# Two MLP layers after a retention layer: the split of the weights' sums put one slot behind the sums, and parts of two x sums put two slots later

## The chip, the cores and the metric

The kernel runs on one core of a Trainium2 chip. The metric is the device time of that core in microseconds (us); smaller is better.

## The reference, cut to what matters

```python
x = retention(q, k, v)                    # 1536 tokens x 512, state over time, 8 heads
h = x @ w_in;   x = softplus(h) @ w_out   # first MLP, d_ff 2048
h = x @ w_in2;  g = s * relu(h)**2 + b
out = g @ w_out2                          # second MLP
```

All data are float32 for the caller. The kernel keeps float32 accuracy on TensorE by splitting each operand into a high part and a low part (hi + lo) and adding three products: hi x hi, hi x lo, lo x hi.

## The kernel before

The kernel has a retention stage, a first MLP layer whose early steps run between the retention's steps, and a second MLP layer. The change concerns the second layer and the passage into it. The tokens are three tiles j = 0, 1, 2 of 512; d_ff is 16 blocks of 128, taken as 8 pairs p. The order of the instructions on every engine is the order in which the program issues them, and an engine takes its instructions strictly in that order.

**Weights.** A weight block arrives packed; `split_w` unpacks one half of it (index 0: w_in, 1: w_out) in steps. DVE runs L286, L290, L295 and L301; ACT runs Square (L293, output `wm`) ahead of L301; then `split` (L109) makes the parts: ACT copies `wh` (L111) and POOL subtracts `wl` (L114). The generator stops between steps, and `go(work, n)` runs n further ones.

**Sums of weights.** For the pairs 1 to 7 the layer's first product over tiles 0 and 1 is made in Strassen's way with seven half-sized products. It needs four sums of the weights (`sums_w`: four POOL instructions on tile `ws`, L320), split into `sh` (ACT, L111) and `sl` (POOL, L114), and sums of x (`sum_x`, DVE, L431 and L435, in place in `xa`), split by `parts_x` (ACT copy at L442 or L445, POOL subtraction at L448).

**Slots.** `halves` lists the pieces in the order in which they are taken: for each pair two w_in halves, the sums, and two w_out halves, five pieces. Each call of `part(p)` takes the next one. Pair 0 is `plain(0)`, six slots, one for each tile and block; this document names them (0,0), (0,1), (1,0), (1,1), (2,0), (2,1). A slot issues the 12 matmuls of the first product (`all_of`), then `flat` and `bend` (ACT: Relu, Square at L491, L492, copy `gh` at L111; POOL: `gl` at L114), then two steps of the piece, then the matmuls and additions given to it (`accs`), then `sum_x` and `parts_x`, then the rest of the piece. In (1,0) `accs` is `end`: the first layer's last accumulation and `take_last`, in which DVE adds (L416), ACT copies (L418) and DVE subtracts (L420). After that the accumulator banks are free, and (1,1) issues the second layer's first accumulation (`acc_2`, L510).

The pairs 1 to 7 are `second(p)`, in six groups of matmuls; the first five had a piece each. This document calls them s1 to s6. In s1 `kept` copies a PSUM bank to tile `p1` on ACT (L468), and `joined` adds on DVE (L479) and applies Relu on ACT (L480). In s2 `kept` fills `p5` and `u2`. `six` issues six matmuls of a half-sized product. There are three banks for these results, `h`, `y` and `third`, and a new product waits for the copy or addition that empties its bank.

Of the kernel before, what the change touches and what calls it, by code (L numbers as in the profile page):

```python
# [47 lines left out]
def tile_retention_mlps(ctx: ExitStack, tc: tile.TileContext, qk, kv, w1, w2, sb, consts, out):  # L48
# [19 lines left out]
    def bank(pool, tag):  # L68
        return pool.tile([P, 512], F32, tag=tag, name=tag)
# [39 lines left out]
    def split(hi, lo, src, hi_eng, lo_eng):  # L109
        if hi_eng is nc.scalar:  # L110
            nc.scalar.activation(hi, src, AF.Copy)  # L111
        else:
            hi_eng.tensor_copy(hi, src)
        lo_eng.tensor_tensor(out=lo, in0=src, in1=hi.bitcast(F32), op=ALU.subtract)  # L114
# [158 lines left out]
    def split_w(w, i, pause):  # L273

        wh = wp.tile([P, DM], F32R, tag=f"wh{i}", name=f"wh{i}")
        wl = wp.tile([P, DM], F32R, tag=f"wl{i}", name=f"wl{i}")
        t = raw_t.pop((w, i))
        lw, hw = t[:, :, 0], t[:, :, 1]

        if bank_2:  # L280
            x = bank_2[w < NF and 1 - i].bitcast(U32)
        else:
            x = (un[:, i] if spare() else word()).bitcast(U32)
        m = dp.tile([P, DM], F32, tag="wm", name="wm")

        nc.vector.tensor_scalar(  # L286
            out=x, in0=hw, scalar1=3, scalar2=0x3FFFFFF8, op0=ALU.logical_shift_left, op1=ALU.bitwise_and
        )
        yield
        nc.vector.scalar_tensor_tensor(  # L290
            out=x, in0=hw, scalar=cu[:, 0:1], in1=x, op0=ALU.bitwise_and, op1=ALU.bitwise_or
        )
        nc.scalar.activation(m, hw.bitcast(F32), AF.Square)  # L293
        yield
        nc.vector.scalar_tensor_tensor(  # L295
            out=x, in0=lw, scalar=cu[:, 1:2], in1=x, op0=ALU.logical_shift_right, op1=ALU.bitwise_or
        )
        load_next()
        yield

        nc.vector.scalar_tensor_tensor(  # L301
            out=m, in0=m, scalar=TINY_SQ, in1=x.bitcast(F32), op0=ALU.is_ge, op1=ALU.mult
        )
        m_t[w, i] = m
        if pause:
            yield
        split(wh, wl, m, nc.scalar, nc.gpsimd)
        w_t[w, i] = (wh, wl)

    def sums_w(w):  # L310

        a, b = m_t[w, 0], m_t[w + 1, 0]
        t = late.tile([P, 4, KH], F32, tag="ws", name="ws")
        for o, x, y, op in (
            (0, b[:, :KH], b[:, KH:], ALU.add),
            (1, t[:, 0], a[:, :KH], ALU.subtract),
            (2, a[:, :KH], b[:, :KH], ALU.subtract),
            (3, a[:, KH:], t[:, 1], ALU.subtract),
        ):
            nc.gpsimd.tensor_tensor(out=t[:, o], in0=x, in1=y, op=op)  # L320
            if o == 1:
                yield
        hi = late.tile([P, 4, KH], F32R, tag="sh", name="sh", bufs=2)
        lo = late.tile([P, 4, KH], F32R, tag="sl", name="sl", bufs=2)
        yield
        split(hi, lo, t, nc.scalar, nc.gpsimd)
        s_t[w] = (hi, lo)


    steps = [(0, g, j, f4) for g in range(NG) for j in range(NTILE) for f4 in range(FG)]  # L330
# [94 lines left out]
    def sum_x(k):  # L425

        (b11, b21), (b12, b22) = ((xa[j][:, 0:2], xa[j][:, 2:4]) for j in (0, 1))
        if k == 3:
            for c, tag in enumerate(("p1", "p5")):
                t = late.tile([P, TT], F32, tag=tag, name=tag)  # L430
                nc.vector.tensor_tensor(out=t, in0=b22[:, c], in1=b12[:, c], op=ALU.subtract)  # L431
                x3.append(t)
            return
        to, x, y = {1: (b11, b12, b11), 2: (b22, b22, b11), 4: (b12, b21, b22)}[k]
        nc.vector.tensor_tensor(out=to, in0=x, in1=y, op=ALU.subtract)  # L435
        x_t[k] = to
# [46 lines left out]
    def flat(ps):  # L483
        c = next_t()
        nc.scalar.activation(c, ps, AF.Relu)
        return c
# [55 lines left out]
        ),  # L542
    )
    for w in range(NF, 2 * NF, 2):
        halves += [(w, 0), (w + 1, 0)] + [(w, 2)] * (w > NF) + [(w, 1), (w + 1, 1)]
    RAWS = 4
    loads, splits = iter([x for x in halves if x[1] < 2]), iter(halves)
    nxt = [next(splits)]
# [6 lines left out]
    def split_next(s):  # L555
        x = nxt[0]
        if x is None or (x[0] < NF + 2 and x[1] < 2 and s < slot_free(*x)) or (NF + 2 <= x[0] and s < NS):
            return iter(())
        assert x[0] >= NF or s + 1 <= first_use(*x) or s <= min(SB, first_use(*x)), (s, x)
        nxt[0] = next(splits, None)  # L560
        if x[1] == 2:
            return sums_w(x[0])
        return split_w(*x, pause=True)

    def go(work, n):
        for _ in range(n):
            next(work, None)
# [57 lines left out]
    with tc.manual_schedule():  # L625
# [119 lines left out]
        def part(p):  # L745
            return split_next(NS + p) if p < PAIRS - 1 else iter(())
# [5 lines left out]
        def plain(p):  # L752

            w = NF + 2 * p

            def slot(j, half, to, accs, sums=(), parts=()):
                work = part(p)
                all_of(to, w_t[w + half, 0], j)
                c = flat(to)
                bend(c, p, half, j)  # L760
                go(work, 2)
                accs()
                for k in sums:
                    sum_x(k)
                for k in parts:
                    parts_x(k)
                go(work, 3)

            def end():
                for banks in (FIRST, SECOND):  # L770
                    acc_mm(NS - 1, banks)
                    take_last(banks)

            def sums_0():
                acc_2(p, 0, 1)
                take(p, 0)

            slot(0, 0, bank(ps_h, "h"), lambda: acc_mm(NS - 3, FIRST + SECOND), sums=(2,), parts=(1,))
            slot(0, 1, bank(ps_y, "y"), lambda: acc_mm(NS - 2, FIRST + SECOND), sums=(4,), parts=(2,))
            slot(1, 0, bank_2[1], end)  # L780
            slot(1, 1, bank(ps_h, "h"), lambda: acc_2(p, 0, 0), parts=(4,))
            slot(2, 0, bank_2[1], sums_0)
            slot(2, 1, bank(ps_y, "y"), lambda: None, parts=(3,))

        def second(p):

            w = NF + 2 * p
            (ah, al), (bh, bl), (sh, sl) = w_t[w, 0], w_t[w + 1, 0], s_t[w]
            a11, a12 = (ah[:, :KH], al[:, :KH]), (ah[:, KH:], al[:, KH:])
            a22 = bh[:, KH:], bl[:, KH:]  # L790
            s1, s2, s3, s4 = ((sh[:, k], sl[:, k]) for k in range(4))
            b11, b21 = ((xh[0][:, k : k + 2], xl[0][:, k : k + 2]) for k in (0, 2))
            b22 = xh[1][:, 2:4], xl[1][:, 2:4]
            t1, t2, t3, n4 = (x_t[k] for k in (1, 2, 3, 4))

            one, other, third = bank(ps_h, "h"), bank(ps_y, "y"), bank_2[1]

            work = part(p)
            six(one, a11, b11, True)
            p1 = kept(one, "p1")  # L800
            six(third, a12, b21, True)
            c11 = joined(third, p1)
            go(work, 2)
            acc_2(p - 1, 1, 0)
            bend(c11, p, 0, 0)
            go(work, 3)

            work = part(p)
            six(other, s1, t1, True)
            p5 = kept(other, "p5")  # L810
            six(one, s2, t2, False)
            u2 = kept(one, "u2")
            go(work, 2)
            acc_2(p - 1, 1, 1)
            take(p - 1, 1)
            go(work, 3)

            work = part(p)
            six(other, s4, b22, False)
            c12 = joined(other, u2)  # L820
            six(one, s3, t3, False)
            c22 = joined(one, p5)
            go(work, 2)
            acc_2(p - 1, 2, 0)
            bend(c12, p, 0, 1)
            bend(c22, p, 1, 1)
            go(work, 3)

            work = part(p)
            six(one, a22, n4, False)  # L830
            c21 = flat(one)
            go(work, 2)
            acc_2(p - 1, 2, 1)
            take(p - 1, 2)
            bend(c21, p, 1, 0)
            go(work, 3)

            work = part(p)
            all_of(third, (ah, al), 2)
            ha = flat(third)  # L840
            go(work, 2)
            acc_2(p, 0, 0)
            bend(ha, p, 0, 2)
            go(work, 3)

            other = bank(ps_y, "y")
            all_of(other, (bh, bl), 2)
            hb = flat(other)
            for banks in (FIRST, SECOND) if p == PAIRS - 1 else (FIRST + SECOND,):
                acc_2(p, 0, 1, banks)  # L850
                take(p, 0, banks)
            bend(hb, p, 1, 2)

        go(work, 4)
        act_3(NS - 1)
# [82 lines left out]
```

## Time and profile before

| | |
|---|---|
| median of 3 runs | 591.48 us (591.41 to 592.08) |
| profiled execution, time | 591.23 us |
| its span, first to last instruction | 589.2 us |
| mean granted TensorE clock | 0.988 |
| PE busy | 569.9 us, 97% of the span |
| DVE, ACT, POOL busy | 419.4, 316.6, 237.6 us |

The granted clock is a share of TensorE's full 2.4 GHz; 0.5 is 1.2 GHz. PE is TensorE's matmuls, PEld its weight loads, DVE VectorE, ACT ScalarE, POOL GpSimd. Times in the views count from the span's start; L111 is line 111 of the kernel. A row of a timeline gives start, duration, engine, line, operation, output and inputs, count, and in brackets the idle time ahead of it and what ended that.

### The profile page before, as it was taken

Reading aid. Unit: us, or ns where it says so; the run is one execution under the profiler, and the core shown is the slowest. Engines: PE = TensorE matmul, PEld = TensorE weight load, DVE = VectorE, ACT = ScalarE, POOL = GpSimd, SP = SyncE. Lnnn points to the kernel's source line nnn. Section 1 sums busy time; section 2 is a strip of 40 time slices with the busy share of each in tenths; the row PEclk is TensorE's granted clock in tenths of the full one; section 3 lists DMA queues with packets and bytes.
Section 4 is the critical chain, followed back from the end, with each engine's and each line's share of the span. In section 5 each row is a group of like instructions: output and inputs, shape, how many; then the busy total and the mean of one; then the engine's idle time right before and its main releaser. Section 6 shows DMA issues by size and latency. Waiting matters only on the chain.

```text
span 589.2 us, 7951 instructions
## 1 busy us (share of the span) xinstructions
PE 569.9 (97%) x2986; PEld 467.4 (79%) x2986; DVE 419.4 (71%) x626; ACT 316.6 (54%) x570; POOL 237.6 (40%) x197
## 2 busy tenths in 40 slices
PE   8999999999999999999999498999999999999997
PEld 7777778888888888888888376888888888888885
DVE  4898767779799997999868385739485766653324
ACT  3655564443323323333535577867767676767460
POOL 3547632121111120111535868474746474735030
PEclk9999999999999999999999798999999999999999
DMA  8985122222122221222212032213122221000005
GB/s 329 416 310 202 52 71 73 72 73 73 36 72 71 72 72 37 71 72 71 73 36 65 7 106 71 78 32 98 48 71 72 71 72 60 14 1 0 1 0 214
DMA packets 14869, 50.57 MB, mean 86 GB/s; under 512 B 1776, under 2 KB 1776, under 8 KB 14832
## 3 DMA queue, kind: packets, MB, share of 16 engines
q1 hardware_dynamic: 14832, 50.08, 24.8%
q8 instruction: 23, 0.38, 0.3%
q14 instruction: 14, 0.11, 0.1%
HBM read 46.93 MB, written 3.15 MB: 85 GB/s over the span
## 4 chain that ended last, share of the span: by engine, by line
PE 82%; DMA 5%; DVE 4%; POOL 3%; ACT 3%; issue 2%; SPq 0%; DVEq 0%; POOLq 0%
PE acc L510 21%; PE acc L396 20%; PE h L349 12%; PE y L349 9%; PE h L454 6%; PE y L462 3%; PE third L462 3%; PE y L454 3%; DMA qk<-qk 3%; PE y L189 2%; DMA raw<-w 2%; PE third L454 1%; PE s L173 1%; POOL gl L114 1%; POOL wl L114 1%
## 5 line engine op out<-in xcount | busy, mean ns | idle before, releaser
L114 POOL TENSOR_TENSOR wl<-wm,wh 128x512 fp32r<-128x512 f32 x64 | 83.3, 1302 | 230.9 <-ACT wh L111 230.8
L519 DVE TENSOR_TENSOR xa<-acc,xa 128x512 f32<-128x512 f32 x84 | 52.4, 683 | 81.6 <-PE acc L510 81.5
L114 POOL TENSOR_TENSOR gl<-c,gh 128x512 fp32r<-128x512 f32 x48 | 63.2, 1316 | 80.8 <-ACT gh L111 67.2
L362 ACT ACTIVATE t<-t 128x512 f32<-128x512 f32 x48 | 30.2, 630 | 102.9 <-DVE t L356 102.8
L510 PE MATMUL acc<-wh,gh 128*128 128x512 f32 x192 | 76.1, 396 | 8.6 <-DVE xl L420 8.6
L510 PE MATMUL acc<-wh,gl 128*128 128x512 f32 x192 | 75.6, 394 | 0.0
L396 PE MATMUL acc<-gh,wh 128*128 128x512 f32 x192 | 75.6, 394 | 0.0
L396 PE MATMUL acc<-gl,wh 128*128 128x512 f32 x192 | 74.8, 390 | 0.0
L111 ACT ACTIVATE wh<-wm 128x512 fp32r<-128x512 f32 x64 | 39.8, 622 | 52.2 <-DVE wm L301 52.2
L396 PE MATMUL acc<-gh,wl 128*128 128x512 f32 x192 | 58.1, 389 | 0.0
L382 DVE TENSOR_TENSOR gl<-t,gh 128x512 fp32r<-128x512 f32 x40 | 51.7, 1293 | 1.2 <-ACT gh L378 1.2
L510 PE MATMUL acc<-wl,gh 128*128 128x512 f32 x192 | 52.5, 389 | 0.0
L510 PEld LDWEIGHTS acc<-wh,gh 128*128 128x128 f32 x192 | 36.5, 190 | 17.5 <-issue 9.0
L293 ACT ACTIVATE wm<-raw 128x512 f32<-128x512 f32 x64 | 42.2, 660 | 8.5 <-POOL wl L114 8.4
L349 PE MATMUL h<-xh,wh 128*128 128x512 f32 x112 | 44.7, 399 | 2.2 <-DVE t L366 1.7
L349 PE MATMUL h<-xl,wh 128*128 128x512 f32 x112 | 43.7, 390 | 0.0
L396 PEld LDWEIGHTS acc<-gh,wh 128*128 128x128 f32 x192 | 36.0, 188 | 8.8 <-DVE xa L406 1.0
L510 PEld LDWEIGHTS acc<-wh,gl 128*128 128x128 f32 x192 | 36.6, 191 | 7.5
L510 PEld LDWEIGHTS acc<-wl,gh 128*128 128x128 f32 x192 | 36.2, 188 | 7.6
L396 PEld LDWEIGHTS acc<-gh,wl 128*128 128x128 f32 x192 | 36.0, 188 | 7.6
L396 PEld LDWEIGHTS acc<-gl,wh 128*128 128x128 f32 x192 | 36.1, 188 | 7.2
L492 ACT ACTIVATE c<-c,sbt 128x512 f32<-128x512 f32 x48 | 39.2, 816 | 1.6
(178 smaller groups left out, 1239.1 us busy)
## 6 DMA issues: line engine op xcount, KB each, us to landing
raw<-w SPq DMA_DIRECT2D x64, 512.0 KB, 3.7
qk<-qk SPq DMA_DIRECT2D x12, 512.0 KB, 8.1
kv<-kv SPq DMA_DIRECT2D x12, 512.0 KB, 8.0
out<-xa SPq DMA_DIRECT2D x12, 256.0 KB, 2.1
cst<-consts SPq DMA_DIRECT2D x1, 518.0 KB, 4.1
cst<-consts SPq DMA_DIRECT2D x1, 256.0 KB, 5.9
sbt<-sb SPq DMA_DIRECT2D x1, 1.0 KB, 9.8
```

What stands on the lines that cost most here:

```text
L111: nc.scalar.activation(hi, src, AF.Copy)
L114: lo_eng.tensor_tensor(out=lo, in0=src, in1=hi.bitcast(F32), op=ALU.subtract)
L293: nc.scalar.activation(m, hw.bitcast(F32), AF.Square)
L349: nc.tensor.matmul(ps, w[:, cc * P : (cc + 1) * P], r[j][:, cc, :], start=i == 0, stop=i == len(ops) - 1)
L362: nc.scalar.activation(l_t[s], l_t[s], AF.Softplus)
L382: (eng or nc.vector).tensor_tensor(out=gl, in0=l_t.pop(s), in1=gh.bitcast(F32), op=ALU.subtract)
L396: nc.tensor.matmul(acc_t[la, g, j][cc], *ops[i], start=f4 == 0 and i == 0, stop=ends(s) and i == 2)
L454: nc.tensor.matmul(ps, w[a][:, k * P : (k + 1) * P], x[b][:, k], start=start and i == 0, stop=i == len(ops) - 1, skip_group_check=True,)
L462: nc.tensor.matmul(ps, w[a][:, k * P : (k + 1) * P], (xh, xl)[b][j][:, k], start=i == 0, stop=i == len(ops) - 1)
L492: nc.scalar.activation(c, c, AF.Identity, scale=sbt[:, 0:1], bias=sbt[:, 1:2])
L510: nc.tensor.matmul(acc_t[1, p, j][cc], *ops[i], start=half == 0 and i == 0, stop=half == 1 and i == 2)
L519: nc.vector.tensor_tensor(out=dst, in0=ps, in1=dst, op=ALU.add)
```

## The change

The split of the sums becomes a piece of its own, so a pair has six pieces, and s6 of `second(p)` gets a piece as well. `sum_x(4)` moves from (0,1) to (0,0), behind `sum_x(2)`. `parts_x(2)` moves from (0,1) to (1,1), and `parts_x(4)` from (1,1) to (2,0). The two halves of the third x sum are kept in the tiles `p5` and `u2` instead of `p1` and `p5`.

```diff
 def sums_w(w):
             nc.gpsimd.tensor_tensor(out=t[:, o], in0=x, in1=y, op=op)
             if o == 1:
                 yield
+        s_t[w] = t
+
+    def split_sums(w):
         hi = late.tile([P, 4, KH], F32R, tag="sh", name="sh", bufs=2)
         lo = late.tile([P, 4, KH], F32R, tag="sl", name="sl", bufs=2)
+        split(hi, lo, s_t[w], nc.scalar, nc.gpsimd)
+        s_t[w] = (hi, lo)
         yield
-        split(hi, lo, t, nc.scalar, nc.gpsimd)
-        s_t[w] = (hi, lo)
...
-            for c, tag in enumerate(("p1", "p5")):
+            for c, tag in enumerate(("p5", "u2")):
...
-        halves += [(w, 0), (w + 1, 0)] + [(w, 2)] * (w > NF) + [(w, 1), (w + 1, 1)]
+        halves += [(w, 0), (w + 1, 0)] + [(w, 2), (w, 3)] * (w > NF) + [(w, 1), (w + 1, 1)]
...
         if x[1] == 2:
             return sums_w(x[0])
+        if x[1] == 3:
+            return split_sums(x[0])
...
-            slot(0, 0, bank(ps_h, "h"), lambda: acc_mm(NS - 3, FIRST + SECOND), sums=(2,), parts=(1,))
-            slot(0, 1, bank(ps_y, "y"), lambda: acc_mm(NS - 2, FIRST + SECOND), sums=(4,), parts=(2,))
+            slot(0, 0, bank(ps_h, "h"), lambda: acc_mm(NS - 3, FIRST + SECOND), sums=(2, 4), parts=(1,))
+            slot(0, 1, bank(ps_y, "y"), lambda: acc_mm(NS - 2, FIRST + SECOND))
             slot(1, 0, bank_2[1], end)
-            slot(1, 1, bank(ps_h, "h"), lambda: acc_2(p, 0, 0), parts=(4,))
-            slot(2, 0, bank_2[1], sums_0)
+            slot(1, 1, bank(ps_h, "h"), lambda: acc_2(p, 0, 0), parts=(2,))
+            slot(2, 0, bank_2[1], sums_0, parts=(4,))
             slot(2, 1, bank(ps_y, "y"), lambda: None, parts=(3,))
...
+            work = part(p)
             other = bank(ps_y, "y")
             all_of(other, (bh, bl), 2)
             hb = flat(other)
+            go(work, 2)
             for banks in (FIRST, SECOND) if p == PAIRS - 1 else (FIRST + SECOND,):
                 acc_2(p, 0, 1, banks)
                 take(p, 0, banks)
             bend(hb, p, 1, 2)
+            go(work, 3)
```

## Rows read from the trace of the kernel before

**Rows 1.** Stretches: us; busy PE, PEld, DVE, ACT, POOL; clock; DMA share; GB/s.

```profile
44.00:48.00 4.00, 3.41 (x20) 2.62 (x22) 3.83 (x8) 2.43 (x7) 3.24 (x3) 1.00 0.71 281
...
365.10:368.70 3.60, 3.60 (x10) 2.80 (x9) 1.39 (x3) 1.49 (x3) 2.46 (x2) 0.53 0.46 146
372.00:556.00 184.00, 184.00 (x813) 152.38 (x812) 111.14 (x170) 128.09 (x205) 99.22 (x82) 1.00 0.15 49
```

**Rows 2.** Timeline of PE, 336 to 372 us.

```profile
337.47 0.77 PE L510 MATMUL acc<-wh,gh 128*128 128x512 f32 x1 [8.58 <-DVE xl L420]
...
342.16 0.39 PE L462 MATMUL third<-xh,wh 128*128 128x512 f32 x1
...
358.00 0.50 PE L454 MATMUL h<-x2h,sh 128*128 128x512 f32 x1 [0.72 <-ACT p L468]
...
364.33 0.50 PE L454 MATMUL y<-xh,sh 128*128 128x512 f32 x1 [1.95 <-ACT p L468]
...
368.77 0.39 PE L510 MATMUL acc<-wh,gh 128*128 128x512 f32 x1
```

**Rows 3.** Timeline of ACT, 320 to 336 us.

```profile
322.23 0.63 ACT L111 ACTIVATE wh<-wm 128x512 fp32r<-128x512 f32 x1 [1.22 <-DVE wm L301]
...
324.89 0.63 ACT L111 ACTIVATE gh<-c 128x512 fp32r<-128x512 f32 x1
...
330.76 1.06 ACT L111 ACTIVATE sh<-ws 128x1024 fp32r<-128x1024 f32 x1 [4.29 <-POOL ws L320]
331.73 0.58 ACT L485 ACTIVATE c<-third 128x512 f32<-128x512 f32 x1
...
334.94 1.07 ACT L418 ACTIVATE xh<-acc 128x512 fp32r<-128x512 f32 x2
```

**Rows 4.** Timeline of DVE, 319 to 326 us.

```profile
319.52 1.22 DVE L435 TENSOR_TENSOR xa<-xa,xa 128x1024 f32<-128x1024 f32 x1
...
322.11 2.11 DVE L435 TENSOR_TENSOR xa<-xa,xa 128x1024 f32<-128x1024 f32 x1
```

**Rows 5.** Timeline of POOL, 319 to 331 us.

```profile
319.56 2.32 POOL L114 TENSOR_TENSOR gl<-c,gh 128x512 fp32r<-128x512 f32 x1 [1.90 <-ACT gh L111]
...
326.59 1.29 POOL L114 TENSOR_TENSOR gl<-c,gh 128x512 fp32r<-128x512 f32 x1
327.83 0.73 POOL L320 TENSOR_TENSOR ws<-wm 128x256 f32<-128x256 f32 x1
```

**Rows 6.** Tile x1l: ns min/median/max of one, first and last start.

```profile
L448 POOL TENSOR_TENSOR x1l<-xa,x1h x2: 1288/1780/2273, 321.9 to 323.1; 128x512 fp32r<-128x512 f32 x2
```

**Rows 7.** Timeline of ACT, 356 to 366 us (s1 and s2 of pair 1).

```profile
357.36 0.60 ACT L468 ACTIVATE p<-h 128x512 f32<-128x512 f32 x1 [0.54 <-POOL xl L448]
358.71 0.63 ACT L480 ACTIVATE c<-c 128x512 f32<-128x512 f32 x1 [0.76 <-DVE c L479]
...
363.70 0.58 ACT L468 ACTIVATE p<-y 128x512 f32<-128x512 f32 x1
```

**Rows 8.** Timeline of ACT, 434 to 470 us (a later pair).

```profile
433.59 0.63 ACT L480 ACTIVATE c<-c 128x512 f32<-128x512 f32 x1
...
436.71 0.62 ACT L491 ACTIVATE c<-c 128x512 f32<-128x512 f32 x1
```

**Rows 9.** Timeline of DVE, 448 to 468 us.

```profile
448.78 2.48 DVE L519 TENSOR_TENSOR xa<-acc,xa 128x512 f32<-128x512 f32 x4 [3.76 <-PE acc L510]
...
464.15 0.68 DVE L479 TENSOR_TENSOR c<-h,p 128x512 f32<-128x512 f32 x1
...
466.25 0.76 DVE L295 SCALAR_TENSOR_TENSOR word<-raw,cu,word 128x512 uint32<-128x512 uint32 x1
467.14 0.69 DVE L301 SCALAR_TENSOR_TENSOR wm<-wm,word 128x512 f32<-128x512 f32 x1
```

**Rows 10.** Chain that ended last, 448 to 462 us: start, us, what.

```profile
460.08 1.36 PE y L454 x6
```

## The prediction

> **What bounds the kernel now.** I read the page's engine totals first, then PE's waits, then the granted clock by stretches, and then each engine's timeline where PE waits. PE is the bound: from 372 to 556 us it is busy all the time at full clock [rows 1], and nothing that shortens another engine there can pay. What is left lies in the passage into the second layer, where PE waits three times [rows 2]: 8.58 us ahead of 337.47, 0.72 ahead of 358.00 and 1.95 ahead of 364.33. After the first and the third wait it runs for a while at half clock. A sequence of 12 matmuls takes 2 x 1.36 = 2.72 us at full clock [rows 10]; from 337.47 to 342.16 it took 4.69, and from 364.33 to 368.77 it took 4.44 [rows 2], with a granted clock of 0.53 in the second stretch [rows 1]. So 1.97 and 1.72 us more. Those five items, 14.9 us, are all that this change can win; the time to lose is in the pairs, where nothing is idle now.
>
> Why PE waits: the first time it wants an accumulator bank that `take_last` empties. Its ACT copy (334.94) stands behind the four instructions of the third slot's bend and a Square, and these stand behind `sh`, which had kept ACT idle for 4.29 us, waiting for `ws` on POOL [rows 3]. The second time `p1` is not written yet, since POOL still reads the third x sum in that same tile: 0.54 us of ACT's idle time [rows 7]. The third time ACT writes `p5` only at 363.70 [rows 7], since its queue has the `sh` of the next pair ahead of it, with its wait for `ws`.
>
> **The change, part by part.**
>
> *First wait.* `sh` is now issued behind the third slot's bend, so these instructions run while ACT would wait for `ws`. From 331.73 to 334.94, 3.21 us, leaves the path behind `sh` [rows 3]; the Square goes with it, because the w_out half is taken a slot later. Against this stands how late `ws` and so `sh` become. `sum_x(4)` now stands ahead of L295 and L301 of the piece in (0,0). Its price: 1.22 or 2.11 us [rows 4]. The traces tell why two sizes: the first sum began 0.04 us before POOL's `gl`, kept its 1.22, and `gl` took 2.32 instead of 1.29; the other began 0.2 us after the first `x1l`, was held back until that ended (1.29), and then the second `x1l`, next on POOL, was held to 2.27 [rows 4 to 6]. So the one that began first runs on, and at its end the waiting one goes before its neighbour's next. `gl` waits when `sum_x(4)` comes, so it should go first, to 319.56 + 2.32 = 321.88, and `sum_x(4)` should end at 321.88 + 1.22 = 323.10. The copy `wh` came 322.23 - 320.74 = 1.49 after the end of the sum; it now comes at 324.59. From `wh` to `gh` is 2.66 [rows 3], so `gh` ends at 327.25 + 0.63 = 327.88. POOL is ready: two `x1l` and a `wl` of 1.29 from 323.10 end by 326.97. `gl` begins at 327.88, `ws` 1.24 later, and `sh` 2.93 after `ws` begins (327.83 to 330.76): 332.05. ACT has done the third bend by then (from 327.8, under 3.21). The next copy comes 0.97 after `sh`: 333.02 instead of 334.94. **1.9 us won.** From that copy to PE is 2.53 as before, so PE resumes near 335.6.
>
> The other bound: if `sum_x(4)` follows its neighbour at 320.74 without giving way, it ends at 321.96 and `wh` comes at 323.45. `gl` then begins at 321.96 and ends at 323.25, two `x1l` and `wl` at 327.12, the second `gl` starts there, `sh` at 331.29, the copy at 332.26: 2.7 us won. I take 1.9, as `x1l` shows the waiting engine served first.
>
> The Trainium skill, page "SBUF — State Buffer", section "Who interferes with whom", says that a DVE instruction with two SBUF inputs contends with a GpSimd instruction that reads SBUF, and that issue order decides which blocks; the durations in [rows 4 to 6] agree. It speaks against two such sums side by side, but does not say who is served when a second one queues: the sum would be 5.4 us with `gl` first and 6.2 with DVE first.
>
> *Half clock after it.* PE is still idle for some 6.7 us, so I leave the 1.97 us as it is.
>
> *The moved parts.* `x2h`/`x2l` take the place of `x4h`/`x4l` in (1,1), same shapes, no difference. `x4h` in (2,0) is one ACT copy of 1.05 us, as `sh` shows for that shape [rows 3]; it runs while ACT waits for DVE, which has to empty four banks there (2.48, as [rows 9]) before L295 and L301. `x4l` is two POOL instructions of 1.29 before a `wl` that PE needs only in pair 1. Without that cover it would cost 1.05 on ACT. Zero, then. The weight loads are issued inside `split_w`, four halves ahead; they come at most a slot later with their consumers.
>
> *Second wait.* `p1` is no longer the third sum's tile, so ACT's 0.54 us goes: **0.54 won**; `p5` and `u2` are written later than POOL's reading ends. 0.2 us of the wait stays.
>
> *Third wait.* In s1 of pair 1 there is now a w_in half where the sums were, and its `wh` stands ahead of `p5`. In times of before: `p1` at 356.82, Relu 1.35 later at 358.17 [rows 7], then Square, bend and the next instruction 3.12 later [rows 8] at 361.29, `wh` (0.63), `p5` (0.58): 362.50. DVE keeps up: its addition follows `p1` (0.60 long), 2.99 later L301 starts, 0.69 long [rows 9]: 361.1. PE would be there at 364.33 - 1.95 - 0.54 = 361.84, and resumes at 362.5: about 0.7 of the 1.95 remain. **1.25 won.** Bounds: nothing of it, and all 1.95.
>
> *Half clock after that.* The two waits left are 0.2 and 0.7 us, some 4 us apart. From 44 to 48 us PE was idle for 0.59 of 4 us with the clock at 1.00 [rows 1]. I take it that the clock stays: **1.72 won**; the bound is nothing.
>
> *Pairs 2 to 7.* ACT and DVE get another order, PE the same. In s6 DVE now has L295 and L301 behind the four additions: 448.78 + 2.48 + 0.89 + 0.69 = 452.94, then `wh` 0.63, `p1` 0.60: 454.2, needed 2.72 + 1.36 ahead of 460.08, at 456.00 [rows 9, 10]. From `p1` (453.57) Relu at 454.92, then 3.12, 0.63 and 0.58 as above: `p5` is ready at 459.25, needed at 460.08 [rows 10]. 0.8 us to spare, so no cost. This is the thinnest cover of the change: beyond 0.8 us, each of the pairs 2 to 6 pays (pair 7 takes no piece).
>
> Sum: 1.9 + 0.54 + 1.25 + 1.72 = 5.4 us. The profiled execution took 591.23 us, 2.0 more than its span, and 0.25 less than the median; 591.48 - 5.4 = 586.1 us.
>
> **The rivals.**
> *The clock falls all the same.* The two short waits left, or a later one, suffice. For it: in the kernel before, full clock held through 0.72 us and fell after 1.95 more. Against it: the 44 to 48 us stretch. Gain 3.7, time 587.8 us. The Trainium skill, page "TensorE: Matmul & The Clock Gate", section "A second HAM failure mode: psum-queue depth-cycling", says that brief idle times between groups of matmuls can make the clock swing; by that this case would hold, and no row here shows it for waits this short.
> *DVE's second sum goes first.* Gain 6.2, time 585.3 us. For it: it is issued as its neighbour ends. Against it: `x1l`.
> *The first wait stays.* `sh` would have to come 3.2 us late, for example with both effects of the contention and a later `ws`. Then 3.5 are won: 588.0 us. POOL's order, with `ws` behind `gl`, is what speaks for it; no row gives 3.2.
> *Slower: `p5` becomes late in each pair.* `wh` of the new piece in s1 now stands ahead of `p5`. If ACT's chain from DVE's four additions to `p5` is longer than reckoned by 0.8 us, PE waits in five pairs. A wait of x each without loss of clock costs 5x, and it decides from x = 1.1, a chain 1.9 us longer; with a fall of the clock each time (1.72) already the first 0.1 us decides. With x = 1.5 and no fall it is 7.5 lost against 5.4 won, 593.6 us; with the falls some 602. For it: the slack is small. Against it: durations in the pairs repeat to 0.1 us.
>
> **How the numbers follow.** The forecast has 0.45, the clock's fall 0.2, DVE first 0.15, the first wait 0.08, the slower case 0.07; 0.05 are for mixtures near no change. A measurement of this kernel tells 0.2% (1.2 us) from no change. Slower by more than that: 0.06, same 0.04, faster 0.90. The predicted time is 586.1 us. The range reaches from DVE first with a smaller third wait (584.5) to the two rivals near 588 with a little more: 588.4.
>
> **What would show it.** In the profile after: no ACT instruction between `sh` and the copy at L418; PE's first wait near 6.7 us; `p1` without a wait for POOL; `p5` behind `wh` rather than `sh`, with PE idle under 1 us ahead of it; granted clock 1.00 behind it; PE without idle time in the pairs 2 to 7. The prediction is wrong if PE waits for `p5` in each pair, if `sum_x(4)` takes over 3 us, or if half clock shows behind the third wait.

## The result, and the profile after

The changed kernel took 586.0 us (median of 4 runs, 585.67 to 586.56) against 591.68 us of the kernel before in the same set of runs: ratio 0.9904, 95% interval 0.9887 to 0.9922. A later set gave 586.16 against 590.73 us: 0.9926, interval 0.9913 to 0.9939. The forecast was 586.1 us. The profiled execution took 586.24 us with a span of 584.2 us, 5.0 less than before.

PE's waits after, from its timeline (they answer to [rows 2]):

```profile
335.56 0.77 PE L513 MATMUL acc<-wh,gh 128*128 128x512 f32 x1 [6.62 <-DVE xl L423]
...
340.88 0.40 PE L465 MATMUL third<-xh,wh 128*128 128x512 f32 x1
...
356.03 0.50 PE L457 MATMUL h<-x2h,sh 128*128 128x512 f32 x1
...
361.02 0.50 PE L457 MATMUL y<-xh,sh 128*128 128x512 f32 x1 [0.62 <-ACT p L471]
...
363.87 0.39 PE L513 MATMUL acc<-wh,gh 128*128 128x512 f32 x1
```

The three waits were 8.58, 0.72 and 1.95 us; they are 6.62, none that the view lists, and 0.62. ACT's timeline shows why (it answers to [rows 3] and [rows 7]; L421 is the copy of `take_last`, L471 `kept`):

```profile
324.52 0.63 ACT L111 ACTIVATE wh<-wm 128x512 fp32r<-128x512 f32 x1 [3.46 <-DVE wm L301]
...
327.19 0.63 ACT L111 ACTIVATE gh<-c 128x512 fp32r<-128x512 f32 x1
...
332.06 1.06 ACT L111 ACTIVATE sh<-ws 128x1024 fp32r<-128x1024 f32 x1 [1.59 <-POOL ws L320]
333.03 1.06 ACT L421 ACTIVATE xh<-acc 128x512 fp32r<-128x512 f32 x2
...
355.39 0.58 ACT L471 ACTIVATE p<-h 128x512 f32<-128x512 f32 x1
...
359.87 0.61 ACT L111 ACTIVATE wh<-wm 128x512 fp32r<-128x512 f32 x1
360.39 0.58 ACT L471 ACTIVATE p<-y 128x512 f32<-128x512 f32 x1
```

Nothing stands between `sh` and the copy any more: 0.97 us from start to start, where it was 4.18 (334.94 - 330.76 in [rows 3]). `sh` itself is 1.3 us later than before, because `wh` comes at 324.52 instead of 322.23. Of these 2.29 us only 1.31 reach POOL's second `gl` (327.90 below, 326.59 in [rows 5]): before, that `gl` stood in POOL's queue behind other work, and now it waits for ACT's `gh`. `p1` starts right behind `wh` without a wait for POOL, and `p5` stands behind a `wh` instead of `sh`.

The two sums of x now in (0,0), by tile on DVE (ns min/median/max, first and last start), and POOL's timeline beside them (they answer to [rows 4] and [rows 5]):

```profile
L438 DVE TENSOR_TENSOR xa<-xa,xa x2: 1218/1708/2199, 319.6 to 320.8; 128x1024 f32<-128x1024 f32 x2
```

```profile
319.62 2.33 POOL L114 TENSOR_TENSOR gl<-c,gh 128x512 fp32r<-128x512 f32 x1 [1.90 <-ACT gh L111]
...
327.90 1.29 POOL L114 TENSOR_TENSOR gl<-c,gh 128x512 fp32r<-128x512 f32 x1 [1.21 <-ACT gh L111]
```

The first sum kept its 1.22 us and held `gl` to 2.33; the second took 2.20, which fits a wait until `gl` ended at 321.95. It did not run at full speed right behind its neighbour.

Busy time and granted clock in three stretches after (us; PE, PEld, DVE, ACT, POOL; clock; DMA share; GB/s):

```profile
335.50:340.80 5.30, 5.24 (x12) 3.85 (x13) 4.75 (x8) 4.65 (x8) 0.88 (x2) 0.51 0.00 0
361.00:365.00 4.00, 3.98 (x17) 3.30 (x18) 3.09 (x6) 1.29 (x3) 3.92 (x6) 1.00 0.20 68
366.00:551.00 185.00, 185.00 (x818) 153.19 (x817) 115.64 (x176) 130.05 (x210) 103.06 (x84) 1.00 0.16 52
```

Half clock stays behind the first wait, is absent behind the third, and the pairs run without idle time on PE, as before.

### The profile page after: what moved, and what is told of

Its sections match the earlier page's. It is cut to its first block, busy times and chain, and to the rows that moved or that the text cites. A ratio compares the mean times of both kernels' runs of the same rounds, so it can differ in the third digit from the quotient of the medians.

```text
span 584.2 us, 7958 instructions
## 1 busy us (share of the span) xinstructions
PE 568.8 (97%) x2986; PEld 466.6 (80%) x2986; DVE 420.7 (72%) x626; ACT 314.8 (54%) x570; POOL 238.1 (41%) x197
## 4 chain that ended last, share of the span: by engine, by line
PE 84%; DVE 7%; ACT 3%; DMA 2%; POOL 2%; issue 1%; SPq 1%; DVEq 0%; POOLq 0%; ACTq 0%
PE acc L513 22%; PE acc L399 21%; PE h L352 12%; PE y L352 9%; PE h L457 6%; PE third L465 4%; PE y L465 3%; PE y L457 3%; PE y L189 2%; DMA kv<-kv 2%; PE third L457 1%; PE s L173 1%; DVE wm L301 1%; DVE xa L438 1%; ACT wh L111 1%
```

## The experiments

The change has three parts: the new piece with its slot, the moves of the x sums, and the new tiles. The first four experiments take these apart; "pieces alone", "moves alone" and "tiles alone" below mean them. These four ran on one chip (before: 590.99 us). `sum_x(4)` later, `take_last` ahead of the bend too, and the two with more work ran on a second (before: 591.25 us). The comparison of three versions side by side and the last order experiment ran on a third (before: 590.73 us). The executions of one kernel spread over 0.3 to 2.8 us, so differences under 0.5 us are told from profiles only.

**Only the new tiles** (the kernel before, one line changed).

```diff
-            for c, tag in enumerate(("p1", "p5")):
+            for c, tag in enumerate(("p5", "u2")):
```

> The kernel before, with the third x sum kept in p5 and u2 and nothing else changed. Queue theory (ACT's order decides): p1 is written 0.54 us earlier, PE's second wait shrinks from 0.72 to 0.2 us, but p5 still stands behind sh, and sh behind ws on POOL, so PE resumes at 364.3 as before and its third wait grows by what the second loses: no difference, 591.5 us. Rival, the sum of the prediction taken term by term: 0.54 us less, 591.0 us.

Measured: 591.26 us, ratio 1.0003 (0.9995 to 1.0012): no difference. In PE's and ACT's timelines of this kernel:

```profile
337.88 0.77 PE L510 MATMUL acc<-wh,gh 128*128 128x512 f32 x1 [8.61 <-DVE xl L420]
...
365.69 0.50 PE L454 MATMUL y<-xh,sh 128*128 128x512 f32 x1 [2.61 <-ACT p L468]
```

```profile
358.07 0.57 ACT L468 ACTIVATE p<-h 128x512 f32<-128x512 f32 x1
...
364.10 1.06 ACT L111 ACTIVATE sh<-ws 128x1024 fp32r<-128x1024 f32 x1 [1.89 <-POOL ws L320]
365.06 0.58 ACT L468 ACTIVATE p<-y 128x512 f32<-128x512 f32 x1
```

The wait for `p1` is gone, and the wait for `p5` has grown from 1.95 to 2.61 us, by what the other lost. As long as `sh` and its wait for `ws` stand ahead of `p5`, the term of 0.54 us is worth nothing: it counts only together with the new piece.

This profile shows a second thing, by stretches:

```profile
338.00:342.10 4.10, 4.10 (x10) 2.88 (x11) 3.90 (x7) 1.51 (x3) 0.00 (x0) 0.50 0.04 7
342.10:344.00 1.90, 1.90 (x6) 1.50 (x5) 1.83 (x3) 1.83 (x4) 1.29 (x1) 0.55 0.72 254
365.70:370.00 4.30, 4.30 (x19) 3.55 (x20) 2.66 (x5) 2.74 (x5) 3.25 (x2) 1.00 0.36 122
```

Half clock lasted about 6 us behind the first wait (under 4.7 in the profile of the kernel before) and did not come behind the third, although that wait was longer than before. The next experiment shows the same.

**Only the moves of x** (the kernel before, with the slots of the kernel after).

```diff
-            slot(0, 0, ..., sums=(2,), parts=(1,))
-            slot(0, 1, ..., sums=(4,), parts=(2,))
-            slot(1, 1, ..., parts=(4,))
-            slot(2, 0, ...)
+            slot(0, 0, ..., sums=(2, 4), parts=(1,))
+            slot(0, 1, ...)
+            slot(1, 1, ..., parts=(2,))
+            slot(2, 0, ..., parts=(4,))
```

> The kernel before, with sum_x(4) in (0,0), parts_x(2) in (1,1) and parts_x(4) in (2,0), and nothing else changed. Queue theory: sum_x(4) makes wh and gl of (0,1) late, ws and sh come 1.3 us later, and the bend still stands behind sh, so PE's first wait grows by 1.3 us to about 9.9; p1 and p5 come another 0.3 us later: 593.1 us. Rival, POOL's load: x2l (2.5 us) no longer stands between ws and sl, POOL is free earlier and the first wait shrinks by up to 2.5 us: 589.0 us.

Measured: 592.2 us, ratio 1.0024 (1.0015 to 1.0033): slower, on the queue theory's side, by 1.2 us where it expected 1.6. Lines of ACT, of PE, and of the stretch behind the third wait:

```profile
332.01 1.06 ACT L111 ACTIVATE sh<-ws 128x1024 fp32r<-128x1024 f32 x1 [4.24 <-POOL ws L320]
...
336.18 1.07 ACT L418 ACTIVATE xh<-acc 128x512 fp32r<-128x512 f32 x2
```

```profile
338.71 0.76 PE L510 MATMUL acc<-wh,gh 128*128 128x512 f32 x1 [9.82 <-DVE xl L420]
...
366.23 0.50 PE L454 MATMUL y<-xh,sh 128*128 128x512 f32 x1 [1.96 <-ACT p L468]
```

```profile
366.20:370.00 3.80, 3.77 (x17) 3.12 (x18) 2.89 (x6) 2.27 (x4) 3.24 (x2) 1.00 0.37 125
```

`sh` is 1.25 us later than in [rows 3], and PE's first wait 1.24 longer, 9.82 us. POOL's relief from `x2l` gives nothing back, since `ws` stood ahead of `x2l`. The further 0.3 us at `p1` and `p5` did not come: the third wait has the size of before, 1.96 us. The clock behind it is at 1.00.

**The pieces without the moves and the tiles** (the kernel after, both taken back).

> The kernel after, without the moves of x and without the new tiles: the split of the sums is a piece of its own, six pieces a pair. Queue theory: sh still comes at 330.8, and the third bend runs ahead of it, so the first wait shrinks by 3.2 us; p1 still waits for POOL; p5 is no longer behind sh: 1.25 us; the clock stays full: 1.72 us. 6.2 us less than before, 585.3 us, so a little faster than the kernel after. Rival, the moves of x and the tiles are part of the gain: slower than the kernel after, 587 us or more.

Measured: 585.13 us, ratio 0.9901 (0.9886 to 0.9916). The new piece and the sixth slot alone give all of the gain. Lines of ACT and PE:

```profile
331.12 1.06 ACT L111 ACTIVATE sh<-ws 128x1024 fp32r<-128x1024 f32 x1 [1.64 <-POOL ws L320]
332.08 1.06 ACT L421 ACTIVATE xh<-acc 128x512 fp32r<-128x512 f32 x2
```

```profile
334.62 0.76 PE L513 MATMUL acc<-wh,gh 128*128 128x512 f32 x1 [5.38 <-DVE xl L423]
...
354.81 0.50 PE L457 MATMUL h<-x2h,sh 128*128 128x512 f32 x1 [0.67 <-ACT p L471]
359.80 0.50 PE L457 MATMUL y<-xh,sh 128*128 128x512 f32 x1 [0.62 <-ACT p L471]
```

The first wait is 3.20 us shorter than before, as expected, and the wait for `p1` is there again.

**The pieces and the tiles, without the moves.**

> The kernel after, without the moves of x. Queue theory: as the pieces alone, with the 0.54 us of p1 as well: 6.7 us less than before, 584.8 us, 1.3 us faster than the kernel after, with PE's first wait 5.4 us. Rival, the moves of x help: slower than the kernel after, over 586 us.

Measured: 585.15 us, ratio 0.9902 (0.9889 to 0.9916). PE's first wait was 5.39 us and no wait for `p1` is listed, as expected; but the time is that of the pieces alone, and its ratio nearly that of the kernel after (0.9904). So the three ran again side by side:

> The kernel after, on one chip with the three others of this set, so that they can be compared with each other. Both theories: 0.990 to 0.991 of before.

> The kernel after, without the moves of x, beside the kernel after on one chip. The profiles have its first wait 1.2 us shorter (5.39 against 6.62). Queue theory: 1.2 us faster than the kernel after, 0.988 of before. Rival, the moves give something back that the wait does not show: within 0.5 us of the kernel after.

> The kernel after, without the moves of x and without the new tiles, beside the others on one chip. Queue theory: p1 waits 0.54 us for POOL again, and nothing hides it, since sh no longer stands ahead of p5: 0.5 us slower than without the moves alone. Rival, the tiles give nothing, as alone: no difference.

Measured: the kernel after 586.16 us (0.9913 to 0.9939 of before), without the moves 585.65 (0.9904 to 0.9932), without the tiles too 585.75 (0.9899 to 0.9925). The profiles repeat the waits (6.62, 5.40 and 5.37 us), but of the 1.2 us that the first wait differs by, the times show 0.5, inside the spread, and of the 0.54 us of `p1` they show 0.1. The moves of x cost time inside the change as far as the wait goes; for the whole time this is only likely. Part of the difference may lie in the half clock behind the first wait, whose length changes between executions of one kernel, as is shown below under "Half clock behind the first wait".

**`sum_x(4)` later** (the kernel after, the sum in (1,1)).

```diff
-            slot(0, 0, ..., sums=(2, 4), parts=(1,))
-            slot(1, 1, ..., parts=(2,))
+            slot(0, 0, ..., sums=(2,), parts=(1,))
+            slot(1, 1, ..., sums=(4,), parts=(2,))
```

> The kernel after, with sum_x(4) in (1,1) instead of (0,0). Contention theory (sum_x(4) in the first slot costs 2.3 us on ACT's wh and holds x1l on POOL): without it wh comes at 322.3, gl of (0,1) follows wl at 325.7, ws begins at 327.0, sh at 329.9, the copy of take_last at 330.9: PE's first wait shrinks from 6.6 to about 4.5 us, 2.1 us less than the kernel after, 583.9 us. Rival (ws is bound by POOL's own queue, not by the sum): the first wait stays at 6.6 us or shrinks by less than 0.5 us: 585.6 to 586.0 us.

Measured: 584.08 us, ratio 0.9877 (0.9863 to 0.9890). ACT and PE:

```profile
329.83 1.06 ACT L111 ACTIVATE sh<-ws 128x1024 fp32r<-128x1024 f32 x1 [1.63 <-POOL ws L320]
330.79 1.06 ACT L421 ACTIVATE xh<-acc 128x512 fp32r<-128x512 f32 x2
```

```profile
333.32 0.77 PE L513 MATMUL acc<-wh,gh 128*128 128x512 f32 x1 [4.44 <-DVE xl L423]
```

The first wait lost 2.18 us against the kernel after, 2.1 expected. So a second sum ahead of L295 and L301 in slot (0,0), which took 2.20 us there, costs its whole length, down to PE.

**`take_last` ahead of the bend too** (the kernel above; `slot` calls `end` behind `flat`).

```diff
                 c = flat(to)
+                if accs is end:
+                    accs()
                 bend(c, p, half, j)
                 go(work, 2)
-                accs()
+                if accs is not end:
+                    accs()
```

> As the kernel with sum_x(4) in (1,1), and in slot (1,0) the first layer's last accumulation and take_last are issued ahead of the bend and of the split of the sums, so that the copies of take_last stand neither behind the bend nor behind sh. Queue theory: the copy runs at about 327, PE resumes near 330, the first wait falls under 2 us, and the clock may stay full behind it; ACT is then 3 to 4 us behind PE, and p1 and p5 are late by about 1.2 and 0.8 us: 579 us, or 581 with half clock. Rival (ACT is the bound of the whole passage, and the wait only moves on): the waits at p1 and p5 grow by what the first wait loses, 583 to 584 us.

Measured: 579.29 us, ratio 0.9797 (0.9783 to 0.9810): 12 us faster than before, the best version here. ACT, PE, and the stretch from 329 us:

```profile
327.18 1.09 ACT L421 ACTIVATE xh<-acc 128x512 fp32r<-128x512 f32 x2 [0.29 <-DVE acc L419]
```

```profile
331.60 0.50 PE L513 MATMUL acc<-wh,gh 128*128 128x512 f32 x1 [0.70 <-DVE xl L423]
...
349.77 0.50 PE L457 MATMUL h<-x2h,sh 128*128 128x512 f32 x1 [0.95 <-ACT p L471]
354.77 0.50 PE L457 MATMUL y<-xh,sh 128*128 128x512 f32 x1 [0.63 <-ACT p L471]
```

```profile
329.00:336.00 7.00, 6.29 (x27) 4.41 (x26) 6.23 (x9) 5.64 (x9) 4.15 (x5) 1.00 0.00 0
```

The first wait is 0.70 us, ahead of the second half of the accumulators; the first half comes without a listed wait. Half clock does not come: the mean granted clock is 0.999 or 1.000 in each of the five executions. Of what is won, 0.95 us turns into a wait for `p1`.

**The same order in the kernel before, without the new piece.**

> The kernel before, with one change: in slot (1,0) the first layer's last accumulation and take_last are issued ahead of the bend. The split of the sums stays in the slot ahead, so sh still stands ahead of the copy. Queue theory: sh at 330.8, Relu, copy at 332.3 instead of 334.9, the first wait 5.9 us: 2.6 us faster than before, 588.5 us. Rival (the order of take_last and bend alone is what matters, not the split): the first wait under 2 us, 582 us.

Measured: 588.76 us, ratio 0.9964 (0.9952 to 0.9976). ACT and PE:

```profile
331.00 1.06 ACT L111 ACTIVATE sh<-ws 128x1024 fp32r<-128x1024 f32 x1 [4.30 <-POOL ws L320]
...
332.44 1.08 ACT L418 ACTIVATE xh<-acc 128x512 fp32r<-128x512 f32 x2
```

```profile
334.99 0.77 PE L510 MATMUL acc<-wh,gh 128*128 128x512 f32 x1 [5.87 <-DVE xl L420]
...
357.05 0.50 PE L454 MATMUL h<-x2h,sh 128*128 128x512 f32 x1 [2.03 <-ACT p L468]
363.37 0.50 PE L454 MATMUL y<-xh,sh 128*128 128x512 f32 x1 [1.95 <-ACT p L468]
...
366.22 0.39 PE L510 MATMUL acc<-wh,gh 128*128 128x512 f32 x1
```

The first wait is 5.87 us, as expected: `sh` alone, ahead of the copy, keeps it. 2.71 us are won there and 1.31 given back at `p1`; the time fell by 2.0, not by the 2.6 expected. The order pays in full only with `sh` behind the copy, as in the kernel above. No half clock came behind the waits of 2.03 and 1.95 us: the 12 matmuls from 363.37 to 366.22 took 2.85 us, where they took 4.44 in the profile of the kernel before.

**More work ahead of `p5` in the pairs 2 to 6** (the kernel after; the copies change no value).

```diff
             bend(c11, p, 0, 0)
             go(work, 3)
+            if 2 <= p < PAIRS - 1:
+                for _ in range(1):      # 3 in the second kernel
+                    nc.scalar.activation(p1, p1, AF.Copy)
```

> The kernel after, with one more ACT copy of p1 onto itself at the end of s1 of the pairs 2 to 6, ahead of p5 in ACT's queue (extra work, no change of values). In the trace after, p5 is ready at 453.9 and PE takes the bank at 455.2, so 1.2 us are to spare. Slack theory: 0.55 us are hidden, 586.0 us. Rival (the pairs are at ACT's limit): 5 times 0.55, 588.8 us, more with half clock.

> As the kernel with one more copy, with three: 1.6 us more ahead of p5. Slack theory: 0.4 us beyond the cover, in five pairs: 2 us, 588.0 us with full clock; 8 us more if the clock falls after each wait. Rival (nothing is there to cover or the cover is larger than 1.6): 586.0 us.

Measured: 586.41 us with one copy, ratio 0.9918 (0.9904 to 0.9931); 591.82 us with three, ratio 1.0007 (0.9998 to 1.0016). With one, PE has no wait in the pairs; with three, from ACT's and PE's timelines and the busy times of the pairs:

```profile
391.07 1.94 ACT L814 ACTIVATE p<-p 128x512 f32<-128x512 f32 x3
392.92 0.58 ACT L471 ACTIVATE p<-y 128x512 f32<-128x512 f32 x1
```

```profile
393.55 0.50 PE L457 MATMUL y<-xh,sh 128*128 128x512 f32 x1 [0.69 <-ACT p L471]
...
425.81 0.50 PE L457 MATMUL y<-xh,sh 128*128 128x512 f32 x1 [0.68 <-ACT p L471]
```

```profile
372.00:548.00 176.00, 172.22 (x755) 141.02 (x754) 112.21 (x168) 130.23 (x212) 97.11 (x81) 1.00 0.16 54
```

The same two matmuls in PE's timeline of the kernel after, where no wait is listed ahead of them:

```profile
392.43 0.39 PE L457 MATMUL y<-xh,sh 128*128 128x512 f32 x1
...
423.71 0.39 PE L457 MATMUL y<-xh,sh 128*128 128x512 f32 x1
```

The three copies put `p5` off by 1.85 us (391.07 to 392.92), not 1.6, and PE waits in each of five pairs, 0.68 or 0.69 us in four of them and 1.05 in the last. The expected 2 us were too small: 5.4 lie between the kernels with one and with three copies, with the clock at 1.00 in that stretch. The busy times show 3.8 of them as idle, but a wait costs more than the idle time that the view lists: that time begins at the end of the last matmul, while matmuls otherwise overlap (0.39 us long, some 0.23 apart). From one of these matmuls to the next it is 32.26 us (393.55 to 425.81), and 31.28 in the kernel after (392.43 to 423.71). So a listed wait of 0.68 us cost 0.98, and counted in this way the five pairs hold 5.3 of the 5.4 us (361.29 to 554.38 with three copies, 361.02 to 548.83 in the kernel after). The cover in the pairs is there, about 1.2 us, and the whole gain of the change is gone if 1.85 us more come ahead of `p5`.

## Why the prediction was right, step by step

**First wait, 1.9 us.** Shown: 8.58 to 6.62. The chain came as reckoned: `sh` at 332.06 (332.05), the copy at 333.03 (333.02), PE at 335.56 (335.6). The two parts of the sum were confirmed one by one: the third bend leaving the path behind `sh` gives 3.20 us (pieces alone), and `sum_x(4)` ahead of L295 costs 1.24 (moves alone) and 1.23 (6.62 against 5.39). The choice that POOL's waiting `gl` goes ahead of DVE's second sum was right: 2.20 us for the sum.

**Second wait, 0.54 us.** Shown within the change: no wait is listed any more, where 0.72 us were, so it was a little more than reckoned. Alone the new tiles are worth nothing, which the prediction did not say: as long as `sh` stands ahead of `p5`, PE only comes to the next wait sooner.

**Third wait, 1.25 us.** Shown: 1.95 to 0.62, so 1.33. The pieces alone give the same (0.62), the tiles alone do not (2.61): it is `sh` leaving the path ahead of `p5`, as said.

**Half clock behind the first wait, left as it was.** 12 matmuls took 5.32 us (335.56 to 340.88) instead of 4.69: 0.63 us worse in the profiled execution. A second profile of the kernel after, from the set side by side, has the same wait and 4.57 us (335.80 to 340.37):

```profile
335.80 0.76 PE L513 MATMUL acc<-wh,gh 128*128 128x512 f32 x1 [6.62 <-DVE xl L423]
...
340.37 0.39 PE L465 MATMUL third<-xh,wh 128*128 128x512 f32 x1
```

So this term moves by 0.75 us between two executions of one kernel.

**Half clock behind the third wait, 1.72 us.** This is the term that was taken from one execution and is not typical of the kernel. Half clock did not come there in the changed kernel, as said: 12 matmuls took 2.85 us (361.02 to 363.87) instead of 4.44. But the profiles of three kernels that keep the third wait at full length (2.61, 1.96 and 1.95 us) did not have it either; in these the half clock behind the first wait had lasted longer. So it is not shown that the shorter wait is what kept the clock up. The kernel before ran 47 times beside the experiments; the mean granted clock was 0.988 in 12 of these and 0.991 in 35. The profile of before has 0.988; the profiles of the tiles alone and of the moves alone, with a long third wait and no half clock behind it, have 0.991. In the set of 21, the median span was 588.9 us at 0.991 and 589.5 at 0.988, a difference of 0.6 and not 1.7; in the set of 15 it was 0.3. So what the change wins in a typical execution is 1.96 + 0.72 + 1.33 us and a little of the clock, near 4.5, as the second set shows (590.73 - 586.16 = 4.57); the first set, with a before of 591.68, showed 5.7. That the forecast of 5.4 us met the first set to 0.1 us in the time is therefore luck in part: the waits gave 4.0 us, where 3.7 were forecast, and the clock some 0.6 in the second set, where 1.72 were forecast. That the 35 executions at 0.991 are of the kind with the longer first half clock is argued from those two profiles; the kernel before itself was profiled only once.

**The sum of the two profiles.** The waits lost 1.96 + 0.72 + 1.33 us, the matmuls behind the first wait took 0.63 more and those behind the third 1.59 less (4.44 - 2.85): 4.97 us, and the spans differ by 5.0. So the whole difference lies in the passage, as the prediction had it.

**The moved parts and the pairs, nothing.** Right. The reserve ahead of `p5` was reckoned as 0.8 us; its sum has a slip (448.78 + 2.48 + 0.89 + 0.69 is 452.84), so its own terms give 0.9. In the pair shown PE began to wait at 393.55 - 0.69 = 392.86, and without the copies `p5` would have been written at 392.92 + 0.58 - 1.85 = 391.65: 1.2 us. The slower rival was a real danger in the right place: one copy more is hidden, three take back 5.4 us. Its price came out right by two errors that cancel: a chain 1.9 us longer was to cost 5.4, and 1.85 did, but with a larger reserve (1.2) and a dearer wait (0.98 us for a listed 0.68).

**The rivals.** The clock's fall behind short waits did not come: 0.62 us left it at 1.00 in the kernel after, and so did five waits of 0.68 to 1.05 us, some 32 us apart, in the kernel with three copies. The rule cited from the Trainium skill, page "TensorE: Matmul & The Clock Gate", section "A second HAM failure mode: psum-queue depth-cycling", is about brief idle times that come often; waits of this size and distance did not bring it about here, and no run shows many of them close together. DVE's second sum did not go first (2.20 us), and `sh` was 1.3 us late, not 3.2.

## What to carry to other kernels

On an engine that takes its queue in order, look for the short instruction that frees the bottleneck's buffer, and count what stands ahead of it; a piece that waits for another engine belongs behind it. Here the split one slot later won 3.2 us at the first wait, putting the copies of `take_last` ahead of both the bend and the split brought that wait from 4.44 to 0.70 us in the kernel with `sum_x(4)` later, and the fix of a smaller wait was worth nothing while a later instruction of the same queue still waited for the same thing. A term that rests on the clock should be read from more than one execution before it goes into a sum. And a wait costs more than its listed idle time: measure from start to start.

## What the runs showed of the hardware

Two float32 sums on DVE with both inputs in SBUF, issued one behind the other, did not keep POOL out for both. By the durations (1.22, then 2.20 us on DVE; 2.33 on POOL, where 1.29 is usual) POOL's waiting instruction went ahead of the second sum, as one DVE sum had come between POOL's two `x1l` [rows 4 to 6]. The Trainium skill, page "SBUF — State Buffer", section "Who interferes with whom", has it that such a pair contends; these durations agree.

Half clock behind a wait of 2 us does not follow from the size of the wait: it came behind 1.95 us in one profile and stayed away behind 1.95, 1.96, 2.03 and 2.61 in those of three other kernels. Behind the first wait it came in every profile with 4.4 us or more of waiting, and it lasted differently in two executions of the same kernel with the same wait (12 matmuls in 5.32 and 4.57 us behind 6.62). With the first wait at 0.70 us it came nowhere.
